# Attention and gated projection on one core: the second products of blocks 3 and 4 move to the end as seven block products for eight, with a new order

## The chip, the cores and the metric

The kernel runs on one core of one Trainium2 chip. The metric is the device time of one execution in microseconds (us), the median of several runs. The engines are named as in the profile: PE is TensorE, DVE is VectorE, ACT is ScalarE, POOL is GpSimd, SP is SyncE, which only issues transfers here.

## The reference

Two layers, all in fp32. The first is an attention whose weights are a sigmoid and not a softmax; the second multiplies a projection of its output with a gate, and projects again:

```
scores = q @ k.T / 8 - log(448)          # batch 8, 12 heads, 448 tokens, 64 per head
x      = sigmoid(scores) @ v             # then (8, 448, 768)
gate   = sigmoid(sum over k<5 of conv_w[k] * x shifted down by 4-k tokens)
out    = (gate * (x @ w_val)) @ w_out    # w_val, w_out: 768 x 768
```

## The kernel before, in words

**Attention.** The 96 heads are 48 *pairs*, and two pairs are one *two* (the index j, 24 of them; `TWOS`). Keys are cut in three chunks of 128 and a rest of 64. For a pair, `scores` (L592) gives three tiles of scores in PSUM, and `scores_rest` (L636) one tile with the rests of both pairs of a two. `attention` applies the sigmoid on ACT (L659); `attend` (L709 for the rests, L717 for the chunks) multiplies with the values. fp32 accuracy comes in one of two ways. A *whole* operand stays fp32, and each product is one fp32 matmul. A *split* operand is a high and a low part, and each product is three faster matmuls; the split of a tile of attention costs one more copy on ACT (L404 through `scaled`) and one subtraction on DVE (L670). `WHOLE` lists the twos whose attention is whole (0 to 8), `WHOLE_SCORES` the pairs whose scores are whole (0 to 14).

**Blocks.** Three twos make a *block*, one batch element: eight blocks, 0 to 7. Block 0 is cut in seven pieces of 64 tokens, one put behind each other block, so that the projections have seven blocks of 512 columns. `after` copies x out of PSUM on ACT, and makes the gate: five taps on ACT, DVE and POOL, the last two added by an accumulating transfer from POOL's queue (`gate<-tap`, L794). `x_split` makes a high and a low part of x (`xs`) with a scale for the block. In blocks none of whose twos is whole (`bounded`), the scale comes from exponents that are there early. In the others it comes from the largest x: `x_max` on DVE, a reduction, a small diagonal on ACT, and two matmuls by ones (`spread`, L813), which stand on PE ahead of the scores of a pair.

**The two projections.** `product("val", b, m)` (L864) is the first: for each of six m, 18 matmuls of 512 columns (six chunks, three terms), 108 in a block. DVE multiplies the result with the gate (`y`, L889 or L896). `product("out", b, m)` is the second, of the same size, with ACT's copy behind it (`y<-ps_m,o_scale`) and its stores; its operand `g` is a high part cast by a transfer from POOL's queue (`g<-y`, L898) and a low part by a subtraction (L409). This is how blocks 1 to 4 go. The blocks in `LATE` (5, 6, 7) are done in another way, at the end: y is written to HBM (`late_y`), loaded again in a tile of 2 x 2 quarters (`late_load`, ring `y4_ring` of one buffer; the trace names the load `y<-late_y`, L912), and `out_forms` makes seven combinations of the quarters, high and low (ring `f_ring` of one buffer; L923, L398, L409). `late_product` (L956) then does a 2 x 2 block product with seven products of half size in place of eight: four segments (`SEGMENTS`), 189 matmuls of 256 columns in a block, and puts the parts together (L404, L973, L968). Block 7 skips the way by HBM. The forms lie in rings of the attention that are free by then: `qk_src`, `qk_hi`, `qk_lo` for the first, third, ... block of `LATE`, the ring `a` for the second, fourth, ... So a block's forms can be made only when the products of the block two places ahead are done.

**The order.** Nothing is ordered by hand. `op(...)` records each operation with its engines, an estimated cost, a priority, what it reads and what it writes. `Plan.issue` then runs through a plan: on each engine the ready operation of the lowest priority goes first, and the instructions are emitted in that order, which on the chip is fixed for each engine. The priorities are made of the numbers of the table `AT`. An operation whose `port` is "VG" is planned so that DVE and POOL don't overlap in it; a POOL operation also waits on the chip for the last such DVE operation that was planned to take over 0.2 us.

Of the kernel before, what the change touches and what calls it, by code (L numbers as in the profile page):

```python
# [14 lines left out]
I32 = mybir.dt.int32  # L15
# [24 lines left out]
WHOLE = {*range(0, 9)}  # L40
WHOLE_SCORES = {*range(0, 15)}
# [40 lines left out]
LATE = (5, 6, 7)  # L82
AHEAD_OF_VAL = 3

FIRST_TOP = 6
SUMS = 12
OWN_BANKS = (6, 7)
# [5 lines left out]
BY_GPSIMD = ()  # L93
# [7 lines left out]
    first=-15.92, step=186.61, val=336.87, val_step=-29.39, out=-1237.15, out_step=257.57, w_max=1518.34,  # L101
    w_split=-860.95, load_qk_first=-201.47, load_qk=-1852.52, load_v=-662.01, split_hi=32.92, split_lo=-1097.78,
    rest_first=3174.29, rest=-1385.28, a_first=-2081.72, a=-74.73, attend=1686.54, v_max=-553.4, v_exp=-1453.48,
    v_split=144.91, x=-3266.86, x_max=-92.19, x_scale=515.03, x_hi=744.75, x_lo=177.24, x_step=2637.25,
    x_early=1120.5, first_max=-2492.59, tap=891.8, scores=8.56, a_rest=-659.37, a_rest_first=766.83,
    tap_first=-340.19, tap_pair=-743.04, tap_step=-330.6, gate=2823.26, product=-1112.74, y=2077.31, g_hi=-1119.86,
    g_lo=-3664.76, o=-3117.03, sums=-1119.35, f=-1154.59, late=-18.26, late_step=909.44, late_load=-912.54,
    pair0=2133.67, pair1=-1429.33, pair2=330.9, pair3=-1211.45, pair4=1377.13, pair5=-3156.16, pair6=297.98,
    pair7=-522.61, pair8=1609.62, pair9=-2397.11, pair10=-676.08, pair11=-98.56, pair12=-2966.57, pair13=-1287.04,
    pair14=1751.28, pair15=-717.37, pair16=545.19, pair17=-2818.83, pair18=-2085.26, pair19=495.26, pair20=75.11,  # L110
    pair21=-2539.24, pair22=-2144.55, pair23=158.2, val0=-2466.55, val1=1919.24, val2=208.28, val3=1536.8,
    val4=-2488.28, val5=-691.86, out0=173.81, out1=2060.89, out2=3408.9, out3=430.48, out4=2535.97, out5=-302.79,
    val_of1=-468.82, val_of2=-2362.91, val_of3=-1477.84, val_of4=1531.79, val_of5=1921.35, val_of6=-402.85,
    val_of7=1707.7, out_of1=-472.42, out_of2=247.7, out_of3=-1251.83, out_of4=-193.95, out_of5=1473.61,
    out_of6=-476.29, out_of7=-1672.61, share=2436.46, w_load=2736.66,
# [39 lines left out]
class Op:  # L155
    __slots__ = ("ways", "prio", "emit", "deps", "n", "start", "end", "eng", "after", "size", "port", "then")

    def __init__(self, n, ways, prio, emit, size, port):
        self.n, self.ways, self.prio, self.emit, self.size, self.port = n, ways, round(prio, 5), emit, size, port
        self.deps, self.after, self.then = set(), None, None  # L160
        self.start = self.end = self.eng = None


class Plan:
# [9 lines left out]
    YIELD = 0.3  # L174
    DMA_RATE = 310e3
# [5 lines left out]
    def op(self, ways, prio, emit, reads=(), writes=(), size=0, port="VG"):  # L181


        o = Op(len(self.ops), ways, prio, emit, size, port)
# [25 lines left out]
    def issue(self):  # L210
# [13 lines left out]
        events, order, bus, port = [], [], 0.0, 0.0  # L224
# [10 lines left out]
        while events:  # L235
# [6 lines left out]
            for e in engines:  # L242
# [19 lines left out]
                cost = o.ways[e]  # L262
                o.eng, o.start = e, t
# [24 lines left out]
def attention_then_gate(  # L288
# [59 lines left out]
    x_exp = ring(sb, 3, [P, 4], I32, "x_exp")  # L348
    o_scale = ring(sb, 3, [P, NC], F32, "o_scale")
# [9 lines left out]
    op = plan.op  # L359

# [70 lines left out]
    def exponent(e, read, cols, prio, po=None, top=V_TOP):  # L431
# [4 lines left out]
        op({"V": 0.06}, prio + 0.2, lambda _: nc.vector.tensor_scalar(  # L436
            cols[0](), cols[0](), float(31 << 23), float(254 << 23), op0=ALU.max, op1=ALU.min), [], e)
        op({"V": 0.06}, prio + 0.4, lambda _: nc.vector.tensor_scalar(
# [27 lines left out]
    def weight_split(n, m, po=None, to=None):  # L466
# [3 lines left out]
        if po is None:  # L470
            po = ps_m.new()
            to = lambda: po()
            reads, emit = weight_sum(n, m)
            op({"P": 0.05}, prio - 1, lambda e: emit(to()), reads, [po])
# [3 lines left out]
        op({"V": 0.06}, prio, lambda _: nc.vector.tensor_scalar(  # L478
# [102 lines left out]
    def scores(i, c, sums=()):  # L581
# [13 lines left out]
        cost = (0.755 if i in WHOLE_SCORES else 0.607) + (0.1 if c != 1 else 0) + (0.09 if c == 0 and i % 2 else 0) + 0.06 * len(sums)  # L595
        return op({"P": cost}, tau(i) + AT["scores"], emit,
                  (sources(i)[:1] if i == c == 0 else sources(i)) + [x for reads, _ in sums for x in reads], [b])
# [4 lines left out]
    def x_bound(b, t):  # L602
# [6 lines left out]
        op({"V": 0.08}, t + 0.1, lambda _: nc.vector.tensor_scalar(  # L609
            col(0), bits(x), bits(y), bits(z), op0=ALU.max, op1=ALU.max), [x, y, z], [e])  # L610
        op({"V": 0.08}, t + 0.2, lambda _: nc.vector.tensor_scalar(
            col(0), col(0), bits(first_top), float(254 << 23), op0=ALU.max, op1=ALU.min), [first_top], [e])
        op({"V": 0.06}, t + 0.3, lambda _: nc.vector.tensor_scalar(
            col(1), col(0), -1.0, float((254 + X_TOP) << 23), op0=ALU.mult, op1=ALU.add), [], [e])

    def scores_rest(j):
# [12 lines left out]
        def emit(e):  # L629
# [4 lines left out]
            for n, to in enumerate(halves):  # L634
# [3 lines left out]
        o = op({"P": (0.99 if m else 0.89) + (0.1 if firsts else 0)}, t + AT["rest_first" if 2 * j < AHEAD else "rest"], emit,  # L638
               [q for n in range(2) for q in st[2 * j + n]["qk_all"]] + ([ones, m] if m else []) + firsts, [b])
        if firsts:  # L640
            op({"V": 0.08}, t + AT["v_exp"], lambda _: nc.vector.tensor_scalar(
                first_top()[:, 1:4], b()[:, 0, S + 1 : S + 4].bitcast(I32), 0x7F800000, None, op0=ALU.bitwise_and), [], [b, first_top], port="")
            op({"V": 0.08}, t + AT["v_exp"] + 0.1, lambda _: nc.vector.tensor_scalar(
# [552 lines left out]
```

## Time and profile before

| | |
|---|---|
| time, median of 3 runs (lowest, highest) | 575.81 us (575.28, 576.5) |
| the profiled execution's own time | 575.5 us |
| span of that execution, first to last instruction | 573.6 us |
| PE busy | 563.7 us, 98% of the span |
| DVE, ACT, POOL busy | 74%, 70%, 42% |
| granted TensorE clock, mean | 0.998 |
| moved by DMA | 107.25 MB, mean 187 GB/s |

How to read it: the span is 1.9 us shorter than the time of the same execution, and the rest lies around the span. All sums in the prediction are made against 575.5 us. A PE matmul shows a duration longer than its step, since matmuls are pipelined; the step is read from the start of one to the start of the next, or from a piece of the chain divided by its count. The same holds for ACT and DVE: the duration of an instruction holds some 0.1 us in which the next one runs already. A row of the chain "7.77 PE ps_m L864 x36" is 36 matmuls that took 7.77 us on the path that ended last. Whole (fp32) matmuls are recorded twice each, so a pair of whole scores (6 matmuls) is a row with x12.

### The profile page before, as it was taken

To read this page: it belongs to the slowest core of one execution; us is meant where nothing else is said; L and a number is where in the kernel's file an instruction comes from. 1 tells how busy PE (TensorE), PEld (TensorE's weight loads), DVE (VectorE), ACT (ScalarE), POOL (GpSimd) and SP (SyncE) were. 2 spreads that over 40 slices of the span, in tenths; PEclk is the share of its full clock that TensorE was granted. 3 is DMA by queue.
4 is the path that set the end of the run, shared out by engine and by line. 5 is a ranking of instruction groups with operands and counts; after the bars stand their busy time and mean duration, and the time that the engine had idled before them with its cause. 6 is when DMAs were issued, how large, how long until landed. Compare 5 with 4: busy or idle time off the path is not lost.

```text
span 573.6 us, 9982 instructions
## 1 busy us (share of the span) xinstructions
PE 563.7 (98%) x3793; PEld 300.6 (52%) x3793; DVE 423.6 (74%) x653; ACT 401.6 (70%) x488; POOL 242.6 (42%) x301
## 2 busy tenths in 40 slices
PE   9999989999999999999999999999999999999996
PEld 4343334454554545545455445455555446865785
DVE  0867998896789775486766778866878999847544
ACT  5788986556987859677686878997889994332221
POOL 0001346866656285365734455545665421400100
PEclk9999999999999999999999999999999999999999
DMA  8987789968586979686495775976787565730122
GB/s 312 360 272 247 223 216 229 218 159 230 186 207 201 300 162 246 161 198 155 109 231 146 205 172 152 219 191 184 204 237 197 137 166 143 188 94 14 61 75 74
DMA packets 48400, 107.25 MB, mean 187 GB/s; under 512 B 15712, under 2 KB 24544, under 8 KB 48352
## 3 DMA queue, kind: packets, MB, share of 16 engines
q1 hardware_dynamic: 33808, 67.19, 34.3%
q0 software_dynamic: 14256, 39.23, 33.6%
q8 instruction: 30, 0.49, 0.3%
q10 hardware_dynamic: 288, 0.20, 0.1%
q14 instruction: 18, 0.15, 0.1%
HBM read 63.52 MB, written 17.90 MB: 142 GB/s over the span
## 4 chain that ended last, share of the span: by engine, by line
PE 89%; ACT 4%; DVE 3%; issue 2%; DMA 1%; POOL 1%; DVEq 0%; ACTq 0%
PE ps_m L864 42%; PE ps_a L592 15%; PE ps_a L717 15%; PE late L956 7%; PE ps_m L956 4%; PE ps_a L636 4%; PE ps_a L709 3%; ACT a_single L659 1%; DMA g<-y 1%; DVE a L670 1%; ACT gate L404 1%; PE ps_m L1023 1%; DVE gate L790 0%; POOL w_form L409 0%; DVE y L896 0%
## 5 line engine op out<-in xcount | busy, mean ns | idle before, releaser
L864 PE MATMUL ps_m<-xs,w_val_hi 128*128 128x512 f16 x504 | 150.1, 379 | 0.6 <-DVE y L896 0.6
L670 DVE SCALAR_TENSOR_TENSOR a<-ps_a,a 128x896 f16<-128x896 f32 x90 | 95.1, 1090 | 29.2 <-ACT a L404 29.0
L659 ACT ACTIVATE ps_a<-ps_a 128x896 f32<-128x896 f32 x105 | 93.2, 911 | 26.6 <-DVE v_exp L649 16.1
L864 PE MATMUL ps_m<-xs,w_val_lo 128*128 128x512 f16 x252 | 95.5, 379 | 0.0
L787 POOL TENSOR_SCALAR tap<-x,cw 128x512 f32<-128x512 f32 x84 | 69.2, 845 | 56.6 <-DVE gate L790 14.1
L409 POOL TENSOR_TENSOR qk_lo<-qk_src,qk_hi 128x448 fp32r<-128x448 f32 x66 | 74.9, 1156 | 29.9 <-DVE gate L790 11.1
L864 PE MATMUL ps_m<-g,w_out_hi 128*128 128x512 f16 x288 | 86.0, 380 | 0.5 <-POOL g L409 0.5
L404 ACT ACTIVATE a<-ps_a 128x896 f16<-128x896 f32 x90 | 80.1, 928 | 0.2
L864 PEld LDWEIGHTS <-w_val_hi 128*128 128x128 f16 x504 | 47.6, 98 | 60.0 <-issue 7.8
L790 DVE SCALAR_TENSOR_TENSOR gate<-x,cw,gate 128x512 f32<-128x512 f32 x84 | 65.3, 798 | 0.5 <-ACT gate L404 0.3
L659 ACT ACTIVATE a_single<-ps_a 128x896 f32<-128x896 f32 x63 | 53.6, 928 | 17.0 <-DVE out_inverse L434 8.5
L794 POOL DMA_DIRECT2D gate<-tap x42 | 38.8, 925 | 50.3 <-DMA gate<-tap 25.4
L864 PE MATMUL ps_m<-g,w_out_lo 128*128 128x512 f16 x144 | 54.6, 379 | 0.0
L717 PE MATMUL ps_a<-a,v_hi 128*64 128x448 f16 x360 | 49.4, 355 | 0.0
L864 PEld LDWEIGHTS <-w_out_hi 128*128 128x128 f16 x288 | 27.0, 98 | 35.0 <-issue 4.3
L717 PE MATMUL ps_a<-a_single,v_src 128*64 128x448 f32 x216 | 42.6, 543 | 0.0
L567 POOL DMA_DIRECT2D qk_hi<-qk x33 | 20.8, 630 | 48.4 <-PE ps_a L592 35.8
L592 PE MATMUL ps_a<-qk_hi 64*128 64x448 f32 x198 | 40.1, 401 | 0.8 <-DVE a_rest L670 0.8
L864 PEld LDWEIGHTS <-w_val_lo 128*128 128x128 f16 x252 | 24.7, 98 | 29.7
L592 PE MATMUL ps_a<-qk_single 64*128 64x448 f32 x180 | 37.2, 553 | 0.2 <-ACT a_single L659 0.2
L592 PE MATMUL ps_a<-qk_lo,qk_hi 64*128 64x448 f32 x198 | 36.3, 362 | 0.0
L592 PE MATMUL ps_a<-qk_hi,qk_lo 64*128 64x448 f32 x198 | 36.3, 362 | 0.0
(144 smaller groups left out, 936.4 us busy)
## 6 DMA issues: line engine op xcount, KB each, us to landing
gate<-tap POOLq DMA_DIRECT2D x42, 512.0 KB, 5.8
qk_src<-qk SPq DMA_DIRECT2D x33, 448.0 KB, 5.0
qk_hi<-qk POOLq DMA_DIRECT2D x33, 416.0 KB, 4.3
v_src<-vs SPq DMA_DIRECT2D x24, 448.0 KB, 4.1
qk_single<-qk SPq DMA_DIRECT2D x14, 448.0 KB, 6.2
out_t<-y SPq DMA_DIRECT2D x24, 224.0 KB, 2.1
w_words<-w_val SPq DMA_DIRECT2D x6, 768.0 KB, 7.9
w_words<-w_out SPq DMA_DIRECT2D x6, 768.0 KB, 4.8
```

Of the source, the lines that this page charges most:

```text
L404: nc.scalar.activation(to, x, AF.Copy, scale=by)
L409: engines[eng].tensor_tensor(to, x, y, op=ALU.subtract)
L592: mm(b()[:, h, :S], k()[rows, at : at + P], q()[rows, :S], start=(n == 0), stop=(n == len(terms(i)) - 1))
L636: mm(b()[to, h, :S], x[n]()[rows, CW:], x[n]()[rows, :S], start=True, stop=True)
L659: nc.scalar.activation(to, b()[:, :, :S], AF.Sigmoid, bias=-math.log(S), scale=1.0 / math.sqrt(D))
L670: op({"V": 1.0}, t + 0.5, lambda e: nc.vector.scalar_tensor_tensor(part(1), p(), A_SCALE, part(0), op0=ALU.mult, op1=ALU.subtract), [b], [ ...
L717: mm(px()[to, p, :S], v()[:, o : o + D], x(st[2 * j + p]["a", c])[:, h, at : at + S], start=(j == 0 and c == 0 and n == 0), stop=(j > 0 an ...
L787: op({"G": TAP_G}, at + AT["tap_step"] * k - AT["tap_first"] + AT["tap_pair"] * p, lambda e, p=p, k=k, tap=tap: nc.gpsimd.tensor_scalar(by ...
L790: op({"V": 0.67}, at + AT["tap_step"] * k + AT["tap_pair"] * p, lambda e, p=p, part=part, k=k: nc.vector.scalar_tensor_tensor(part(), x()[ ...
L794: op({"G": 1.1}, at + AT["tap_step"] * k, lambda e, tap=tap: nc.gpsimd.dma_start(g(), tap(), accum_op=ALU.add), [tap], [g], 4 * P * T * 4, "")
L864: mm(po()[:, cs], w()[:, c, :], x(k)[:, cs], start=(c == 0 and j == 0), stop=(c == NC - 1 and j == 2))
L956: mm(po()[:, i * HT : (i + 1) * HT], weights(w, k, c), gv[b, c][g]()[:, x, :], start=(c == 0 and i == 0 and j == 0), stop=(c == UNITS - 1 ...
```

## The change

- `LATE` grows from blocks 5 to 7 to blocks 3 to 7. `product("out")` is left for blocks 1 and 2. Segments of the first late block use ring `ps_m`, all others `ps_a`; before, that was block 5, now block 3.
- Two 13 (in block 4) becomes whole, and so do the scores of pair 16 (in two 8). Block 4 is thereby no longer `bounded`: its scale comes from the largest x.
- One-column DVE operations get `port=""` (`narrow`): the plan no longer keeps them apart from POOL. POOL operations now wait for the last DVE operation with `port="VG"` of any planned length.
- The plan's costs on PE change by some hundredths of a us, and changing from one shape of matmul to another gets a cost of its own (`form`, `LEAVE`, `ENTER`).
- Three weights listed in `BY_GPSIMD` get their low half in another way: ACT scales in place and copies, and DVE or POOL subtracts.
- The rings `x_exp` and `o_scale` have 8 buffers, not 3. All numbers of `AT` are new.

```diff
-WHOLE = {*range(0, 9)}
-WHOLE_SCORES = {*range(0, 15)}
+WHOLE = {*range(0, 9), 13}
+WHOLE_SCORES = {*range(0, 15), 16}
...
-LATE = (5, 6, 7)
+LATE = (3, 4, 5, 6, 7)
 AHEAD_OF_VAL = 3
+FIRST_OUT = min({*range(1, B)} - {*LATE}, default=B - 2)
-OWN_BANKS = (6, 7)
...
-BY_GPSIMD = ()
+BY_GPSIMD = (("out", 3), ("out", 5), ("val", 3),)
...
-    first=-15.92, step=186.61, val=336.87, val_step=-29.39, out=-1237.15, out_step=257.57, w_max=1518.34,
+    first=1564.19, step=536.35, val=1468.75, val_step=6875.3, out=4116.12, out_step=3023.8, w_max=-13597.73,
...
+    LEAVE = {"full": 0.0, "wide": 0.095, "tall": 0.098, "small": 0.0}
+    ENTER = {"full": 0.008, "wide": 0.1, "tall": 0.03, "small": 0.0}
...
+                if e == "P":
+                    if o.form != form:
+                        cost += self.LEAVE[form] + self.ENTER[o.form]
+                    form = o.form
...
-    x_exp = ring(sb, 3, [P, 4], I32, "x_exp")
-    o_scale = ring(sb, 3, [P, NC], F32, "o_scale")
+    x_exp = ring(sb, 8, [P, 4], I32, "x_exp")
+    o_scale = ring(sb, 8, [P, NC], F32, "o_scale")
...
+    def narrow(*of):
+        return op(*of, port="")
...
-        op({"V": 0.06}, prio + 0.2, lambda _: nc.vector.tensor_scalar(
+        narrow({"V": 0.06}, prio + 0.2, lambda _: nc.vector.tensor_scalar(
...
-            po = ps_a.new(lambda: ps.tile([P, 512], F32, name="late", tag="ps_a", bufs=ps_a.n)) if b in OWN_BANKS else ps_m.new()
+            po = ps_a.new(lambda: ps.tile([P, 512], F32, name="late", tag="ps_a", bufs=ps_a.n)) if b != LATE[0] else ps_m.new()
...
-        if b == 2:
+        if b == FIRST_OUT + 1:
             weight_scales("out")
-            x_unscale(1)
-        if b > 1:
+            for n in range(1, b):
+                x_unscale(n)
+        if b > FIRST_OUT:
...
-            elif o.eng == "V" and o.ways["V"] > 0.2:
+            elif o.eng == "V":
                 last = traced
```

Counted in the order of the two kernels, on PE: matmuls of 512 columns by `w_out` go from 432 to 216, matmuls of 256 columns of the late products from 567 to 945. On ACT the copies `y<-ps_m,o_scale` go from 24 to 12, the copies of late parts from 18 to 30, the casts of forms from 18 to 30. On POOL's queue the casts `g<-y` go from 24 to 12. On SP's queue the writes of `late_y` go from 12 to 24, the loads of them from 6 to 12.

What moves is seen at three places. **ACT in the second half of the attention**, behind the copy of two 18's x; before (`a` is a split tile of attention, `ps_a` the sigmoid in place, `y` the copy behind a second product):

```order
L404 ACTIVATE v_hi<-v_src,v_exp 128x896
L404 ACTIVATE a<-ps_a 128x2x448
L404 ACTIVATE y<-ps_m,o_scale 128x512
L404 ACTIVATE gate<-x,cw 128x512
L659 ACTIVATE ps_a<-ps_a 128x2x448 x2
L404 ACTIVATE a<-ps_a 128x2x448 x2
L404 ACTIVATE y<-ps_m,o_scale 128x512
L659 ACTIVATE ps_a<-ps_a 128x2x448
L404 ACTIVATE gate<-x,cw 128x512
L404 ACTIVATE a<-ps_a 128x2x448
L796 ACTIVATE gate<-gate 128x1024
L404 ACTIVATE y<-ps_m,o_scale 128x512
```

and in the change, at the same place:

```order
L415 ACTIVATE v_hi<-v_src,v_exp 128x896
L415 ACTIVATE a<-ps_a 128x2x448
L807 ACTIVATE gate<-gate 128x1024
L670 ACTIVATE ps_a<-ps_a 128x2x448 x2
L415 ACTIVATE a<-ps_a 128x2x448 x2
L670 ACTIVATE ps_a<-ps_a 128x2x448
L415 ACTIVATE gate<-x,cw 128x512
L415 ACTIVATE a<-ps_a 128x2x448
L415 ACTIVATE gate<-x,cw 128x512
L670 ACTIVATE ps_a<-ps_a 128x2x448
L415 ACTIVATE xs<-x,x_exp 128x1024
L415 ACTIVATE a_rest<-ps_a 128x2x448
```

The copies of second products are gone from here, and the same work of the attention stands closer together.

**PE ahead of the scores of pair 31** (in two 15), where block 4 ends; before, a second product stands there:

```order
L864 MATMUL ps_m<-g_2885,w_out_hi_96 128x512
L864 LDWEIGHTS w_out_lo_108
L864 MATMUL ps_m<-g_2885,w_out_lo_108 128x512
L592 MATMUL ps_a<-qk_hi 128x448 x2
L592 MATMUL ps_a<-qk_hi,qk_lo 128x448 x2
```

and in the change a first product, and then the two matmuls by ones of block 4's scale:

```order
L875 LDWEIGHTS w_val_lo_107
L875 MATMUL ps_m<-xs,w_val_lo_107 128x512
L824 LDWEIGHTS ones
L824 MATMUL ps_a<-diagonal,ones 128x64
L824 LDWEIGHTS ones
L824 MATMUL ps_a<-diagonal,ones 128x64
L603 MATMUL ps_a<-qk_hi 128x448 x2
L603 MATMUL ps_a<-qk_hi,qk_lo 128x448 x2
```

The scores of pair 31, and all that follows on PE, now stand behind `diagonal`, which ACT makes.

**SP's queue at the end**; before (the second number of `late_y` is the third of the projection, the last one the tensor: 72 to 74 are block 5, 75 to 77 block 6):

```order
L912 DMA y_4950<-late_y_1_73 128x1024
L891 DMA late_y_0_75<-y 128x512 x2
L912 DMA y_5112<-late_y_2_74 128x1024
L891 DMA late_y_1_76<-y 128x512 x2
L912 DMA y_5219<-late_y_0_75 128x1024
L891 DMA late_y_2_77<-y 128x512
L912 DMA y_5287<-late_y_1_76 128x1024
L891 DMA late_y_2_77<-y 128x512
L1001 DMA out_t<-parts 128x2x448
L1001 DMA out_t<-parts 128x2x64
L912 DMA y_5434<-late_y_2_77 128x1024
```

and in the change (72 to 74 are block 3, 75 to 77 block 4, 78 to 80 block 5, 81 to 83 block 6):

```order
L923 DMA y_4966<-late_y_1_76 128x1024
L1012 DMA out_t<-parts 128x2x448
L1012 DMA out_t<-parts 128x2x64
L923 DMA y_5115<-late_y_2_77 128x1024
L1012 DMA out_t<-parts 128x2x448
L1012 DMA out_t<-parts 128x2x64
L923 DMA y_5207<-late_y_0_78 128x1024
L1012 DMA out_t<-parts 128x2x448
L1012 DMA out_t<-parts 128x2x64
L1012 DMA out_t<-parts 128x2x448
L1012 DMA out_t<-parts 128x2x64
L923 DMA y_5329<-late_y_1_79 128x1024
```

The loads now alternate with the stores of finished products: a block's y is loaded while the block before it is being multiplied.

## Rows read from the trace of the kernel before

**Rows 1.** The page: busy time, share of the span and instructions of each engine, and the granted TensorE clock in 40 slices (9 is 90% or more).

```profile
PE 563.7 (98%) x3793; PEld 300.6 (52%) x3793; DVE 423.6 (74%) x653; ACT 401.6 (70%) x488; POOL 242.6 (42%) x301
...
PEclk9999999999999999999999999999999999999999
```

**Rows 2.** All waits of PE: what waited, for whom, us in total, times, the longest.

```profile
PE ps_a L813 <- ACT diagonal L404: 1.3, 1, 1.3
PE ps_m L1023 <- DVE ones L1016: 1.1, 1, 1.1
PE ps_a L592 <- DVE a_rest L670: 0.8, 1, 0.8
PE ps_m L864 <- DVE y L896: 0.6, 1, 0.6
PE ps_m L864 <- POOL g L409: 0.5, 1, 0.5
PE ps_a L633 <- ACT a_single L659: 0.3, 1, 0.3
PE ps_a L636 <- ACT a_single L659: 0.3, 1, 0.3
PE ps_a L592 <- ACT a_single L659: 0.2, 1, 0.2
```

**Rows 3.** The chain that ended last, from 60 to 92 us, in order of time: start, us, what. L709 and L717 are the whole attend of a two, L592 x12 the whole scores of a pair.

```profile
68.04 0.75 PE ps_a L709 x8
68.79 4.68 PE ps_a L717 x24
...
86.75 2.46 PE ps_a L592 x12
```

**Rows 4.** The same chain from 400 to 455 us: one two of the split attention, from its rest scores (L636) to the next.

```profile
412.43 0.91 PE ps_a L636 x8
413.34 0.57 PE ps_a L709 x12
413.91 3.53 PE ps_a L717 x36
417.44 2.03 PE ps_a L592 x18
419.46 5.29 PE ps_m L864 x24
424.75 2.03 PE ps_a L592 x18
426.78 2.70 PE ps_m L864 x12
...
429.48 0.91 PE ps_a L636 x8
```

**Rows 5.** The same chain from 505 to 574 us: 36 matmuls of 512 columns, 276 late matmuls of 256 columns, and what follows PE's last.

```profile
509.37 7.77 PE ps_m L864 x36
...
538.25 30.27 PE late L956 x276
...
568.54 0.75 DVE parts L968
```

**Rows 6.** PE in order of time, about 77 and 309 us: start, us, engine, line, operation, [idle before, and what ended it].

```profile
77.38 0.22 PE L813 MATMUL ps_a<-diagonal,ones 128*128 128x64 bf16 x2 [1.29 <-ACT diagonal L404]
77.53 0.65 PE L592 MATMUL ps_a<-qk_single 64*128 64x448 f32 x2
...
309.12 0.17 PE L631 MATMUL ps_a<-vm,ones 128*128 128x1 bf16 x1
309.21 0.98 PE L636 MATMUL ps_a<-qk_src 64*64 64x448 f32 x8
```

**Rows 7.** Three stretches: length, busy time and instructions of PE, PEld, DVE, ACT and POOL, granted clock, DMA's share, GB/s. The first is six twos of the split attention, from rest scores to rest scores; the second the densest stretch of ACT; the third the late products beside the rest of the first products.

```profile
331.67:447.95 116.28, 116.28 (x841) 61.22 (x844) 90.32 (x132) 101.57 (x123) 66.01 (x82) 1.00 0.76 196
439.67:472.82 33.15, 32.33 (x214) 16.46 (x216) 31.27 (x44) 32.80 (x40) 13.27 (x17) 1.00 0.61 158
472.82:538.25 65.43, 65.43 (x476) 43.79 (x465) 44.88 (x72) 21.68 (x27) 10.01 (x11) 1.00 0.39 101
```

**Rows 8.** ACT's groups in the first of these stretches (331.67 to 447.95 us): busy us, mean ns, idle before them and what ended it.

```profile
L659 ACT ACTIVATE ps_a<-ps_a 128x896 f32<-128x896 f32 x42 | 37.3, 913 | 9.4 <-DVE v_exp L649 6.4 <-PE ps_a L592 2.9
...
L404 ACT ACTIVATE x<-ps_a,v_exp 128x896 f32<-128x896 f32 x6 | 6.0, 1006 | 5.3 <-PE ps_a L717 5.3
...
L404 ACT ACTIVATE y<-ps_m,o_scale 128x512 f32<-128x512 f32 x6 | 4.2, 695 | 0.1
```

**Rows 9.** The loads of late y on SP's queue in order of time, 460 to 500 us.

```profile
467.96 0.32 SPq L912 DMA_DIRECT2D y<-late_y  x1
...
476.88 0.32 SPq L912 DMA_DIRECT2D y<-late_y  x1
...
484.65 0.32 SPq L912 DMA_DIRECT2D y<-late_y  x1
...
494.99 0.34 SPq L912 DMA_DIRECT2D y<-late_y  x1
```

**Rows 10.** Two groups of DVE over the whole span: a six-column operation with `port="VG"`, and a one-column one.

```profile
L831 DVE TENSOR_SCALAR o_scale<-o_base,x_exp 128x6 f32<-128x6 f32 x7 | 6.0, 857 | 0.1
...
L829 DVE TENSOR_SCALAR x_exp<-x_exp 128x1 f32<-128x1 f32 x7 | 1.0, 145 | 0.0
```

More of the change, by code (lines that the diff above doesn't have):

```diff
@@ new lines @@
+    w_split=4887.09, load_qk_first=19087.91, load_qk=22652.0, load_v=-10027.13, split_hi=1393.39, split_lo=-2273.26,
+    rest_first=28009.33, rest=-1368.78, a_first=-13044.74, a=-15086.09, attend=-22955.31, v_max=-10769.23,
+    v_exp=-31213.73, v_split=-3170.55, x=-22099.28, x_max=18978.65, x_scale=1030.85, x_hi=6026.59, x_lo=8531.41,
+    x_step=5071.56, x_early=6465.83, first_max=11567.01, tap=1132.59, scores=13759.23, a_rest=-17835.52,
+    a_rest_first=10628.9, tap_first=10241.68, tap_pair=742.46, tap_step=-1737.78, gate=7569.71, product=3755.81,
@@ L155, with __init__ @@
 class Op:
-    __slots__ = ("ways", "prio", "emit", "deps", "n", "start", "end", "eng", "after", "size", "port", "then")
-    def __init__(self, n, ways, prio, emit, size, port):
+    __slots__ = ("ways", "prio", "emit", "deps", "n", "start", "end", "eng", "after", "size", "port", "then", "form")
+    def __init__(self, n, ways, prio, emit, size, port, form):
         self.n, self.ways, self.prio, self.emit, self.size, self.port = n, ways, round(prio, 5), emit, size, port
+        self.form = form
         self.deps, self.after, self.then = set(), None, None
@@ L179, in __init__, with op @@
         self.ops = []
-    def op(self, ways, prio, emit, reads=(), writes=(), size=0, port="VG"):
-        o = Op(len(self.ops), ways, prio, emit, size, port)
+    def op(self, ways, prio, emit, reads=(), writes=(), size=0, port="VG", form="full"):
+        o = Op(len(self.ops), ways, prio, emit, size, port, form)
         self.ops.append(o)
@@ L223, in issue @@
         held = dict.fromkeys(engines)
-        events, order, bus, port = [], [], 0.0, 0.0
+        events, order, bus, port, form = [], [], 0.0, 0.0, "full"
         def release(o, t):
@@ L636, in emit @@
                     mm(b()[to, h, :S], x[n]()[rows, CW:], x[n]()[rows, :S], start=True, stop=True)
-        o = op({"P": (0.99 if m else 0.89) + (0.1 if firsts else 0)}, t + AT["rest_first" if 2 * j < AHEAD else "rest"], emit,
-               [q for n in range(2) for q in st[2 * j + n]["qk_all"]] + ([ones, m] if m else []) + firsts, [b])
+        o = op({"P": (0.9 if m else 0.805) + (0.09 if firsts else 0)}, t + AT["rest_first" if 2 * j < AHEAD else "rest"], emit,
+               [q for n in range(2) for q in st[2 * j + n]["qk_all"]] + ([ones, m] if m else []) + firsts, [b], form="small")
         if firsts:
@@ L719, in chunks @@
                            skip_group_check=True)
[L721 removed]
+        steps = [op({"P": 0.861 if single else 0.677}, t, rest, [s["a"], *values], [px], form="small")] if j else []
         for p in range(2):
             for cs in ((0, 1), (2,)):
[L724 removed]
+                cost = (0.752 if single else 0.567) * len(cs)
                 steps.append(op({"P": cost}, t, lambda e, p=p, cs=cs: chunks(p, cs),
[L726 removed]
+                                [*(st[2 * j + p]["a", c] for c in cs), *values], [px], form="tall"))
         if not j:
[L728 removed]
+            steps.append(op({"P": 0.861}, t, rest, [s["a"], *values], [px], form="small"))
         for a, b in zip(steps, steps[1:]):
```

62 lines of the change are left out of this document (27 added, 35 removed).

## The prediction

> **What bounds the kernel now.** I read the page first: PE is busy 98% of the span at full clock, every other engine at most 74% [rows 1]. A busy PE alone proves nothing, since matmuls overlap in it, so the second view is the list of PE's waits. All eight together are 5.1 us [rows 2], of which 1.1 is the start. PE thus stands still for 4.0 us of 573.6 once it runs. The third view is the chain in order of time, which gives the price of PE's work in steps, free of the overlap [rows 3 to 5]. The reader is to see that time here is PE's work plus a few waits: what PE no longer has to do is gained, unless new waits take it back. So the sum has two halves: what the change does to PE's work, and who could be late where PE's work gets less.
>
> **The sum**, against the profiled execution's 575.5 us (0.3 under the median of the three, 575.81).
>
> *Second products of blocks 3 and 4.* 432 less 216 is 216 matmuls of 512 columns gone. 36 of them take 7.77 us [rows 5], 0.2158 each, so 46.6 us go. 945 less 567 is 378 late matmuls of 256 columns added. 276 take 30.27 us [rows 5], 0.1097 each, so 41.5 us come. Net **-5.1**. Eight products of the old size would have been 432 in place of 378: the 54 that are missing are the gain, less a little because two matmuls of 256 columns cost 0.219 and one of 512 costs 0.216.
>
> A rule speaks against this. The Trainium skill ("TensorE: Matmul & The Clock Gate", section "Back-to-back issue gap") gives for a sustained stream some 81 ns a matmul of 128 columns and 131 ns of 512. Between them an estimate from that page is some 98 ns for 256 columns, three quarters of the long one and not half, by which the two blocks would lose 8.8 us and not gain 5. The rows above decide against it here: the ratio is 0.1097 to 0.2158.
>
> *Pair 16 with whole scores.* 2.46 us [rows 3] for 2.03 [rows 4]: **+0.4**. It saves POOL a split and a transfer; POOL is not on the path there.
>
> *Two 13 whole.* Its attend takes 0.75 + 4.68 [rows 3] for 0.57 + 3.53 [rows 4]: +1.3. The small matmul for the largest v goes, 0.09 by the starts 309.12 and 309.21 [rows 6]: **+1.2** together. ACT and DVE lose some seven copies and seven subtractions there; it is one two, and cover, not path.
>
> *Block 4's scale.* Two matmuls by ones, 0.15 by the starts 77.38 and 77.53, **+0.15**. They also stand ahead of pair 31's scores, behind a chain from the last x of the block over DVE and ACT. Of the two such places now one waits 1.29 us [rows 6] and the other not at all [rows 2]; those are the bounds, and I take the mean, **+0.65**. Queued behind them is all of PE.
>
> *Edits that I price at nothing.* The order on PE changes its shape of matmul about as often as before, so no switching time is added or saved. One-column DVE operations took 145 ns already, against 857 for the six-column one that keeps `port="VG"` [rows 10]: the chip did not hold them back, so freeing them in the plan moves places in the order, no duration. POOL's added waits on short DVE operations stand on an engine that is busy 42% [rows 1]. The three weights of `BY_GPSIMD` add a copy of under 1 us each on ACT, early, beside PE; if that cover were gone, up to 1 us each. More scale buffers only remove waits. On POOL's queue twelve casts `g<-y` go. On SP's, twelve writes and six loads come and 24 stores of y go against twelve of parts; all are covered by PE's work, the loads with the exception below.
>
> Without new waits: 575.5 - 5.1 + 0.4 + 1.2 + 0.15 + 0.65 = 572.8.
>
> **The attention gets denser: the disputed term.** While the attention lasts, second products were filler for PE in which ACT and DVE could catch up. With blocks 3 and 4 gone, the order has 288 first-product matmuls in the eight twos from the attend of two 15 to that of two 23, 36 each. The last full two of [rows 4] has just that, 24 and 12, and takes 17.05 us (412.43 to 429.48). The six twos of the first stretch take 19.4 us each now [rows 7]. ACT's work in them is 101.57 / 6 = 16.9 us a two, of which 4.2 / 6 = 0.7 are second products' copies that go [rows 8]: 16.2 us of 17.05, **95%**. DVE has 90.32 / 6 = 15.1 (88%), POOL 11.0 (65%), DMA 76% of a longer time [rows 7]. Nothing exceeds PE, but ACT has only 0.85 us a two to wait in.
>
> What that costs is bounded thus. From below: nothing, for PE was busy in all of 116.28 us with ACT at 87%, and one two at the new density is among them. From above: the densest stretch, ACT 32.80 of 33.15 us, where PE lost 0.82 [rows 7]; over 8 x 17.05 = 136.4 us that is 3.4 us, of which 0.8 is in the time already, so +2.6. ACT's 95% lies nearer to the dense stretch. But casts of forms stood in the queue there, and most of these come later in the new order, so I take **+0.5**.
>
> **The end.** The late products need their forms. A block's three sets are made one after the other, through one buffer for y and one for f. The loads of y were issued at 467.96, 476.88, 484.65 and 494.99 [rows 9], 7.8 to 10.3 us apart, 9.0 in the mean. Block 5's sets can start when block 3's products are done, and have as cover block 4's 189 late matmuls (20.7 us) and, by the order, 39 of the first products (8.4 us), 29.1 together. Three sets take 23 to 31 us, 27 in the mean: covered, with up to 1.8 us open. Block 6's have block 5's products and 72 first-product matmuls, 36 us. ACT and DVE are no limit there, at 33% and 69% in the third stretch [rows 7]. I take nothing. After PE's last matmul the same work follows as now [rows 5].
>
> Forecast: 572.8 + 0.5 = **573.3 us**, 2.5 under the median.
>
> **The rivals.**
> - *ACT becomes the bound in the eight twos* (slower). For it: ACT idled 14.7 / 6 = 2.45 us a two in the first stretch, 1.07 of that waiting for DVE's exponent of v, 1.4 for PE [rows 8]. If ACT must wait over 0.85 us a two, it sets the pace. With only the 1.07 a two takes 17.3. With all 2.45 it takes 18.65, 1.6 more eight times, 12.8 us in all. With half of that, 0.8 a two, the time is 572.8 + 6.4 = 579.2. Against it: waits for PE shrink when PE is no longer ahead, and ACT ran 33 us with hardly a gap [rows 7]. Slower than before from 0.5 us a two on. Chance 0.15.
> - *The forms come late* (about no change). Each set costs 10.3 us, as the slowest did, and block 5's products wait 1.8 us; with the upper bounds of the dense stretch half taken, 572.8 + 1.8 + 1.3 = 575.9. Single y loads were never this often on the path, and the loads now stand behind stores in SP's queue, each waiting for a product. Chance 0.16.
> - *Long matmuls are cheaper by the column than the short ones* (the page's rule). At three quarters of 0.2158, 0.162, 378 cost 61.2 us and the net is +14.6 and not -5.1: 593. The late stretch at 0.1097 rules it out. Chance 0.01.
> - *The new order also removes waits.* The waits of [rows 2] stand at seven places whose neighbours all move. If half of the 4.0 us and block 4's wait go, 572.8 - 2.0 - 0.65 - 0.15 = 570.0. It is on the forecast's side; chance 0.15.
> - That the change doesn't do what it says is excluded by the counts in the order (945 and 216).
>
> **How the numbers follow.** Forecast within its bounds 0.53, fewer waits 0.15: faster **0.68**, where faster means over 0.2%, 1.15 us, about what a measurement can tell here. Late forms 0.16: **same**. ACT 0.15 and the page's rule 0.01: slower **0.16**. The range goes down to 570.3, near the case with fewer waits, and up to 577.3, past the late forms (575.9) and both upper bounds of the sum (572.8 + 0.65 + 2.6 = 576.1), short of most of ACT's case.
>
> **What the next profile would show.** Right: the L875 group of `w_out` falls to 216 matmuls and the late ones rise to 945 at the same steps (0.216 and 0.11). The late stretch, from the last attend on, lasts some 150 us and has no PE wait over 1 us. PE's waits total 4 to 6.5 us, and ACT is over 93% busy from about 285 to 420 us. Wrong: PE's waits over 9 us. If they are on ACT or on `a`'s subtraction between 285 and 420 us, the first rival is right, if on the forms after that, the second. If PE's work itself, without waits, doesn't fall by about 3.3 us, the prices are wrong.

## The result: 1% slower, and the profile after

The changed kernel takes 581.82 us, the kernel before 575.75 on the same chip: ratio 1.0103, interval 1.008 to 1.0126. The forecast was 573.3, with a range up to 577.3. The profiled execution took 582.57 us, 7.1 more than that of before.

First the page after: busy time by engine, and the granted clock in 40 slices. It answers to [rows 1].

```profile
PE 565.1 (97%) x3934; PEld 315.3 (54%) x3934; DVE 442.0 (76%) x691; ACT 407.6 (70%) x496; POOL 243.0 (42%) x294
...
PEclk9999999999999999999989999999999999999999
```

PE's busy time didn't fall, although work was taken from it. But busy PE hides steps that are longer than usual, so the steps come next. The chain after, from 504 to 560 us (start, us, what), answers to [rows 5]:

```profile
503.95 15.28 PE late L967 x140
519.23 7.77 PE ps_m L875 x36
...
536.41 23.69 PE late L967 x217
```

0.1091 and 0.1092 us a late matmul of 256 columns, 0.2158 one of 512: the prices of the forecast, and the counts are as forecast. Then all waits of PE, which answer to [rows 2]:

```profile
PE ps_a L603 <- DVE a L681: 2.8, 2, 1.7
PE ps_a L824 <- ACT diagonal L415: 2.1, 1, 2.1
PE ps_a L647 <- ACT a_single L670: 1.5, 1, 1.5
PE ps_m L875 <- DVE y L900: 1.1, 3, 0.4
PE ps_m L1034 <- DVE ones L1027: 1.1, 1, 1.1
PE ps_m L967 <- DVE parts L979: 0.6, 1, 0.6
PE ps_m L967 <- ACT parts L415: 0.5, 1, 0.5
PE ps_a L603 <- ACT a_single L670: 0.4, 1, 0.4
PE ps_a L603 <- DVE a_rest L681: 0.2, 1, 0.2
PE ps_m L967 <- DVE y L900: 0.2, 1, 0.2
```

10.5 us in all, where [rows 2] has 5.1. To split the time fully I add up, from the starts in the trace, what each of PE's steps takes beyond the usual step of its kind, where that is 0.07 us or more. These are the *stalls*; the rest of the time from PE's first matmul to its last is its *work*:

| us | first to last | work | stalls | to 100 us | 100 to 270 | rest of the attention | behind it |
|---|---|---|---|---|---|---|---|
| before | 567.5 | 561.8 | 5.6 | 3.0 | 0.7 | 1.9 | 0.1 |
| after | 574.3 | 559.2 | 15.2 | 5.6 | 0.2 | 6.5 | 2.8 |

The attention ends at 476 us before and 429 after; the border between the last two columns is put at 475 and 432 us. **The work fell by 2.6 us, where 3.35 was forecast (-5.1 + 0.4 + 1.2 + 0.15); the stalls rose by 9.5, where 1.15 was.**

The longest stall of the attention, in PE's order of time (start, us, operation, [idle before, and what ended it]):

```profile
292.95 0.37 PE L603 MATMUL ps_a<-qk_lo,qk_hi 64*128 64x448 f32 x2
295.06 0.47 PE L603 MATMUL ps_a<-qk_hi 64*128 64x448 f32 x2 [1.74 <-DVE a L681]
...
295.86 1.03 PE L875 MATMUL ps_m<-xs,w_val_hi 128*128 128x512 f16 x2
296.69 0.63 PE L875 MATMUL ps_m<-xs,w_val_lo 128*128 128x512 f16 x1
297.12 1.06 PE L875 MATMUL ps_m<-xs,w_val_hi 128*128 128x512 f16 x2
```

The third tile of a pair's scores waits for a place in PSUM, which is free when DVE has subtracted the split of an older tile. Behind the wait the first products go at 0.43 us a matmul, twice the usual step: the clock stands at its lower level, 1.2 GHz, for some 3 us. The row of that stretch (PE, PEld, DVE, ACT, POOL, granted clock, DMA, GB/s) and that of PE's first wait for y:

```profile
296.00:297.00 1.00, 1.00 (x3) 0.30 (x2) 1.00 (x2) 1.00 (x2) 0.61 (x2) 0.50 0.71 274
435.60:450.12 14.52, 13.59 (x74) 6.97 (x72) 14.33 (x18) 5.59 (x7) 6.73 (x9) 1.00 0.78 188
```

The low clock adds 1.6 us to the wait. In the other row DVE is busy 99%, half of it with the gate's taps:

```profile
L801 DVE SCALAR_TENSOR_TENSOR gate<-x,cw,gate 128x512 f32<-128x512 f32 x8 | 7.1, 904 | 0.0
```

Beside these 7.1 us it has 4.0 of splits of x, 3.0 of y and 1.1 of combinations for the first late block, and y, for which PE waits, stands in this queue.

What led to the wait at 293 us is seen in the chain before it:

```profile
289.00 0.90 DVE xs L854
...
290.12 0.59 DVE a L681
...
291.12 1.08 DVE a L681
292.19 0.66 DVE y L900
292.85 0.42 DVE v_lo L701
293.27 0.56 issue
293.83 1.09 DVE a L681
294.93 0.14 issue
295.06 0.87 PE ps_a L603 x6
```

DVE goes from splits of x to subtractions, y and the low part of v. The "issue" at 293.27 isn't idle time of DVE: by the timeline it works on the low part of v until the last subtraction starts. ACT's copy for that subtraction came first (start, us):

```profile
292.27 0.93 ACT L415 ACTIVATE a<-ps_a 128x896 f16<-128x896 f32 x1
292.77 1.14 DVE L701 SCALAR_TENSOR_TENSOR v_lo<-v_src,v_exp,v_hi 128x896 f16<-128x896 f32 x1
```

The copy was done at 293.20 and the subtraction began at 293.83. So some 0.6 us of the wait is DVE's queue; how much of the rest is ACT's isn't seen here.

### The profile page after: what moved, and what is told of

The parts are those of the page before. It is cut to its first block, busy times and chain, and to the rows that moved or that the text cites. A ratio compares the mean times of both kernels' runs of the same rounds, so it can differ in the third digit from the quotient of the medians.

```text
span 580.8 us, 10312 instructions
## 1 busy us (share of the span) xinstructions
PE 565.1 (97%) x3934; PEld 315.3 (54%) x3934; DVE 442.0 (76%) x691; ACT 407.6 (70%) x496; POOL 243.0 (42%) x294
## 4 chain that ended last, share of the span: by engine, by line
PE 73%; DVE 10%; ACT 10%; issue 4%; DMA 1%; POOL 0%; DVEq 0%; ACTq 0%; SPq 0%
PE ps_m L875 26%; PE late L967 14%; PE ps_a L603 12%; PE ps_a L728 12%; ACT ps_a L670 4%; PE ps_a L647 3%; ACT a L415 3%; PE ps_m L967 2%; DVE a L681 2%; PE ps_a L720 2%; DVE gate L801 2%; DVE y L900 1%; DMA y<-late_y 1%; ACT gate L415 1%; DVE forms L420 1%
## 5 line engine op out<-in xcount | busy, mean ns | idle before, releaser
L681 DVE SCALAR_TENSOR_TENSOR a<-ps_a,a 128x896 f16<-128x896 f32 x84 | 88.8, 1085 | 27.5 <-ACT a L415 27.4
L670 ACT ACTIVATE ps_a<-ps_a 128x896 f32<-128x896 f32 x98 | 87.7, 920 | 14.4 <-DVE v_exp L660 11.3
L415 ACT ACTIVATE a<-ps_a 128x896 f16<-128x896 f32 x84 | 74.9, 936 | 0.0
L670 ACT ACTIVATE a_single<-ps_a 128x896 f32<-128x896 f32 x70 | 59.2, 927 | 11.1 <-PE ps_a L720 4.4
L967 PE MATMUL late<-forms,w_form 128*128 128x256 f16 x432 | 58.0, 273 | 0.0
L967 PEld LDWEIGHTS <-w_form 128*128 128x128 f16 x540 | 52.8, 98 | 8.1 <-issue 0.7
L415 ACT ACTIVATE parts<-late,o_scale 128x512 f32<-128x512 f32 x24 | 16.4, 687 | 47.9 <-PE late L967 47.9
L984 DVE TENSOR_TENSOR parts<-parts 128x256 f32<-128x256 f32 (+1 forms) x58 | 27.2, 491 | 27.4 <-ACT parts L415 26.9
L875 PE MATMUL ps_m<-g,w_out_hi 128*128 128x512 f16 x144 | 42.9, 379 | 0.0
L967 PE MATMUL late<-forms,w_out_hi 128*128 128x256 f16 x216 | 38.8, 273 | 0.0
```

The lines of the kernel that those rows point to most:

```text
L415: nc.scalar.activation(to, x, AF.Copy, scale=by)
L670: nc.scalar.activation(to, b()[:, :, :S], AF.Sigmoid, bias=-math.log(S), scale=1.0 / math.sqrt(D))
L681: op({"V": 1.0}, t + 0.5, lambda e: nc.vector.scalar_tensor_tensor(part(1), p(), A_SCALE, part(0), op0=ALU.mult, op1=ALU.subtract), [b], [ ...
L875: mm(po()[:, cs], w()[:, c, :], x(k)[:, cs], start=(c == 0 and j == 0), stop=(c == NC - 1 and j == 2))
L967: mm(po()[:, i * HT : (i + 1) * HT], weights(w, k, c), gv[b, c][g]()[:, x, :], start=(c == 0 and i == 0 and j == 0), stop=(c == UNITS - 1 ...
L984: op({"V": 0.07 + 0.00104 * k, "G": 0.1 + 0.0021 * k}, t, lambda e: engines[e].tensor_tensor(to(), x(), z(), op=ALU.add), reads, [buf])
```

## The experiments

Three theories: **O**, the new order makes the waits, and another order is free of them; **D**, the attention has become too dense for ACT and DVE; **P**, short DVE operations now hold POOL back. The kernel before, measured beside each run, took 575.2 to 575.8 us.

### POOL's waits

e4 undoes the last edit of the diff alone; the order stays.

```diff
-            elif o.eng == "V":
+            elif o.eng == "V" and o.ways["V"] > 0.2:
                 last = traced
```

> The changed kernel in its own order, where POOL operations wait for the last DVE operation that was planned over 0.2 us, as before the change, and no longer for short ones. Theory P: the waits of POOL delay taps and low parts, and the time falls by 2 to 6 us. Theories O and D: POOL is busy 42% and not in front of PE; the time stays within 0.7 us.

582.4 us (1.0119, interval 1.0101 to 1.0138), the waits as in the changed kernel. P falls.

### Operations moved at single places

e1, e2, e3 and e7 emit the planned list with a few operations at other places:

```diff
-    for o in plan.issue():
+    for o in moved(plan.issue()):
```

e1 moves ten (two first taps behind sigmoids, `diagonal` ahead of a sigmoid, the exponents ahead of taps, x's copy earlier), e2 20, e3 19, e7 two (`v_hi` and `v_lo` at 291 to 294 us), e11 those of e1, e2 and e3 together, but for two (47).

> The changed kernel, with ten operations of ACT, DVE and POOL in the first 100 us issued at other places (casts of weights and taps behind the sigmoids and behind the scale of block 1); PE's order and all work stay. Theory O (the lost time is waits that the new order makes, each at its place): the waits on the diagonal (2.1 us) and on the rest scores (1.5 us) fall below 1 us together, and the time falls by 2.0 to 3.5 us against the changed kernel. Theory D (only the thinner cover of the attention behind 285 us costs time): it falls by under 1 us, since a gain so early is waited away later. Theory P (short DVE operations that now hold POOL cost the time): no change, within 0.7 us.

> The changed kernel, with 20 operations of ACT, DVE and POOL between 255 and 432 us at other places (splits of x, taps and low parts of v behind the attention's own subtractions); PE's order and all work stay. Theory O: the waits of scores on a's subtraction (1.7 and 1.1 us) go, the clock holds at 1.00 behind 295 us, and the time falls by 3.5 to 6 us: 3 to 4 of waits and 1.7 of the low clock. Theory D: ACT and DVE are short of time in this stretch whatever their order, the waits turn up at other pairs, and the time falls by 0 to 1.5 us. Theory P: no change, within 0.7 us.

> The changed kernel, with 19 operations of ACT, DVE and POOL between 425 and 480 us at other places (y's product ahead of the splits of x and the taps, the parts' copy ahead of the forms); PE's order and all work stay. Theory O: the waits on y (1.1 us), on the first forms and on the parts (1.6 us) shrink to about 1 us, and the time falls by 1.5 to 3 us. Theory D: it falls by under 1 us, since the places lie behind the dense stretch and its delay remains. Theory P: no change, within 0.7 us.

> The changed kernel with two operations moved, both at its longest wait after 100 us, that of scores on a's subtraction at 293 to 295 us: on ACT the high part of v (v_hi) and on DVE its low part (v_lo) are issued behind the third split of a and no longer ahead of it. Theory O: the wait of 1.7 us falls below 0.5 us, the low clock behind it goes, and the time falls by 1.5 to 3.3 us. Theory D: this wait shrinks, but what was passed over is late at the next products with v or the next scores; the time falls by under 0.7 us.

> The changed kernel with the moves of the early, the middle and the late place together (47 operations of ACT, DVE and POOL; PE and SP keep their order). Theory O: the three gains add up: 1.9 + 1.8 + 0.4 us gives 577.7 us, and up to 2 us more where a wait that one of them pushed on is taken away by the next; 575.5 to 578. Theory D: the middle keeps its wait of about 1.7 us and its low clock, and the time stays at 578 us or above.

| | us | ratio, interval | stalls: to 100 us | 270 to 432 | behind |
|---|---|---|---|---|---|
| changed | 581.82 | 1.0103, 1.008 to 1.0126 | 5.6 | 6.5 | 2.8 |
| e1 | 579.88 | 1.0082, 1.0068 to 1.0095 | 4.7 | 4.9 | 2.8 |
| e2 | 580.04 | 1.0086, 1.0069 to 1.0103 | 6.6 | 5.3 | 2.6 |
| e3 | 581.43 | 1.0101, 1.0085 to 1.0116 | 5.7 | 5.1 | 3.2 |
| e7 | 580.97 | 1.0093, 1.008 to 1.0106 | 5.8 | 5.0 | 2.9 |
| e11 | 581.22 | 1.0117, 1.0095 to 1.0139 | 7.6 | 5.3 | 3.2 |

No interval lies clear of the changed kernel's. Against its median e1 gains 1.9 us, just short of theory O's range, e2 1.8, between the two theories, and e3 0.4, as D expected. The named waits of e1 did shrink where they were aimed at; PE's waits in e1:

```profile
PE ps_a L628 <- DVE a L706: 2.8, 2, 1.8
PE ps_a L628 <- ACT x L434: 1.9, 1, 1.9
...
PE ps_a L672 <- ACT a_single L695: 0.6, 1, 0.6
PE ps_a L849 <- ACT diagonal L440: 0.5, 1, 0.5
```

3.6 us on the diagonal and the rest scores became 1.1, but a new wait of 1.9 on a copy of x stands some 10 us later. By the chain, that copy needs a place in x's ring, which DVE frees with the split of an older x, and this stands behind its taps and the casts of weights. e2 missed the wait at 293 us (1.7 again) and cut that at 385 to 0.2. e7 cut the one at 293 to 0.7, and 0.6 turned up three us later, on PE's small matmul for the largest v (the 1.1 in the first row is the wait at 384 us, which e7 left alone):

```profile
PE ps_a L627 <- DVE a L705: 1.8, 2, 1.1
294.11 0.47 PE L627 MATMUL ps_a<-qk_hi 64*128 64x448 f32 x2 [0.69 <-DVE a L705]
...
PE ps_a L666 <- DVE a L705: 0.6, 1, 0.6
```

The stall of 1.91 us became 0.85 + 0.79. The stretch gained more (1.5 us), since the low clock followed the wait on the diagonal here and is in the first column. That most of the delay only moved is D's expectation; the time fell by 0.85 us, between D's 0.7 and O's 1.5, and not clear of the noise. In e3 the waits on y went (1.1 to 0.4), and the one on the parts' copy grew from 0.5 to 1.6. e11 shows that the gains don't add: its profiled execution has two stretches of low clock.

### Whole orders made anew

e5 and e6 replace the order of both kernels by one in which, by the durations of their traces, fewer operations wait; in e9 and e10 only ACT and DVE change, by five places at most.

> The changed kernel with all its operations, issued in another order on PE, ACT, DVE and POOL over the whole span (found by moving operations a few places so that, with the durations of the trace, fewer wait). SP's queue keeps its order. Theory O (the lost time is the order's, and the smaller work of PE is there to be had): PE's waits fall from 10.3 to under 4 us, the low clock at 295 us goes, and the time is 568 to 573 us, under the kernel before. Theory D (with the second products of blocks 3 and 4 gone, ACT and DVE can't keep up from 285 to 430 us in any order): waits of 3 to 5 us and the low clock stay there, and the time is 575 to 579 us.

> The kernel before, its order treated in the same way with the durations of its own trace. Both theories: its waits of 5.1 us fall to under 3 us and its time by 2 to 5 us, to 571 to 573.5 us. Theory O: the changed kernel treated so lies 1 to 3.5 us below this one, by the work that PE no longer has. Theory D: it lies above this one by 3 us or more.

> The changed kernel with all its operations; PE, POOL and SP keep their order, so that no transfer from POOL's or SP's queue changes places, and ACT and DVE issue theirs at most five places earlier or later (127 of 496 and 253 of 689 moved, so that by the trace's durations fewer wait). Theory O: the waits at 76 to 84 us, at 293 and 385 us and at 438 to 470 us shrink from 10 us together to 4 us or less, and the time is 569 to 574 us, below the kernel before. Theory D: about 3 us of waits stay between 285 and 430 us, those outside go, and the time is 575 to 578 us. If the moves only push the waits on, as in the reordering that also moved POOL and PE, the time is above 580 us.

> The kernel before, treated in the same way: PE, POOL and SP keep their order, ACT and DVE issue theirs at most five places earlier or later by its own trace's durations. Both theories: its 4 us of waits inside the run shrink to 1 to 2 us, and the time is 571 to 574 us. Theory O: the changed kernel treated so lies within 2 us of this one or below it. Theory D: it lies 3 us or more above it.

621.9, 606.0, 591.5 and 590.4 us (ratios 1.082, 1.054, 1.0285 and 1.0247): all far slower, and they decide nothing between O and D. Moving POOL's operations moved its transfers. In e5 the low parts of q and k wait for their high parts' transfer, 19 times:

```profile
POOL qk_lo L550 <- DMA qk_hi<-qk: 62.9, 19, 7.0
```

In e9 and e10 no transfer changes its place in its queue; why they lose as much isn't shown.

### Less work for DVE

e8 skips, in the same order, the 41 taps that DVE adds between 262 and 445 us:

```diff
     for o in plan.issue():
+        if o.n in SKIP:
+            continue
         o.emit(o.eng)
```

> The changed kernel in its own order without the 41 taps that DVE adds to the gate between 262 and 445 us (33 us of DVE; the gate lacks them). PE, ACT and POOL keep their work. Theory D, with DVE as the short engine: the waits on a's subtraction (2.8 us) and on y (1.1 us) and the low clock go, and the time falls by 4 to 6 us. With ACT as the short engine: only the waits that DVE's queue made by itself go, and the time falls by 0.5 to 2.5 us. Theory O says the same as the second: what is left waits for ACT in its order.

579.74 us (1.0071, interval 1.0058 to 1.0084). Its row of 285 to 425 us has DVE at 73% and ACT at 94%, and the waits on `a` are still there:

```profile
285.00:425.00 140.00, 136.72 (x1017) 71.97 (x1015) 102.60 (x150) 131.50 (x160) 80.75 (x101) 1.00 0.78 205
```

```profile
PE ps_a L608 <- DVE a L686: 3.0, 3, 1.6
...
PE ps_m L880 <- DVE y L905: 0.4, 1, 0.4
```

So DVE's taps don't make these waits. What stands ahead of the subtraction that ends the longest of them:

```profile
292.23 0.93 ACT L420 ACTIVATE a<-ps_a 128x896 f16<-128x896 f32 x1
292.50 1.14 DVE L706 SCALAR_TENSOR_TENSOR v_lo<-v_src,v_exp,v_hi 128x896 f16<-128x896 f32 x1
293.56 1.08 DVE L686 SCALAR_TENSOR_TENSOR a<-ps_a,a 128x896 f16<-128x896 f32 x1
```

ACT's copy was done at 293.16, so 0.4 of the 1.6 us is the low part of v on DVE, and the rest points to ACT, which worked without a gap from 287.24 us on. The stalls behind the attention fell from 2.8 to 1.2 us, and those were DVE's queue.

### Parts of the change alone, and other densities

Here the order is planned anew from the table's numbers. e12 is the kernel before with `LATE = (3, 4, 5, 6, 7)` and what this needs; e13 and e17 are the changed kernel with three and four late blocks, e14 without two 13 and pair 16 whole, e15 and e16 with one two more whole (e15 to e17 in two executions each). The edit of e13:

```diff
-LATE = (3, 4, 5, 6, 7)
+LATE = (5, 6, 7)
```

> The kernel before with one part of the change alone: the second products of blocks 3 and 4 go to the end as well (LATE of five blocks, the rings and scales that this needs); numbers, costs and the whole twos stay as they were, and the order follows from the old numbers. PE's work falls by 5.1 us. Theory D: without that filler ACT and DVE are late all over the second half of the attention, and the time is 578 to 590 us. Theory O: the new numbers made the loss; with the old ones waits rise by less than 5 us and the time is 570 to 576 us.

> The changed kernel with three late blocks (5 to 7), as before the change, and all its other edits and numbers. PE has 5.1 us of work more, and the second products of blocks 3 and 4 are back as filler. Theory D: the waits between 285 and 430 us go, and the time is 576 to 581 us, below the changed kernel in spite of the longer work. Theory O: the new numbers make waits here too, and the time is 583 to 592 us.

> The changed kernel without two 13 and pair 16 among the whole ones: PE's work is 1.7 us shorter by the rows of before (0.4 + 1.2 + 0.15), ACT and DVE have seven more copies and subtractions about 340 us, and the order follows from the same numbers. Theory D: ACT has even less time there, waits rise by more than PE saves, and the time is 581 to 586 us. Theory O: the time is 577 to 581 us, or anything if the order falls out otherwise.

> The changed kernel with two 14 whole as well (in block 4, whose scale comes from the largest x already). PE +1.2 us, ACT and DVE seven copies and seven subtractions less just ahead of the dense stretch. If relief of ACT there is what counts (theory D), the waits on a's subtraction fall below the 2.8 us of the changed kernel and the time is 578 to 582 us. If what counts is that the numbers were made for one set of operations (theory O), they rise to over 8 us and the time is 588 to 598 us, as for the other kernels whose order followed anew from the numbers.

> The same with two 17 in place of two 14 (in block 5, which thereby takes its scale from the largest x: two matmuls by ones more). PE +1.4 us, ACT's relief lies inside the dense stretch. Theory D: 577 to 582 us. Theory O: 588 to 600 us.

> The changed kernel with four late blocks (4 to 7): the second product of block 3 is back as filler, PE has 2.55 us of work more. By theory D ACT's share in 285 to 425 us falls from 93% to about 88% and the waits on a's subtraction to about what the kernel with three late blocks had (3.5 us) or less. By theory O the time is 585 to 600 us all the same, with waits elsewhere; by theory D alone it is 576 to 583 us.

The stretch from 285 to 425 us, in the kernels before, after and e12 (columns as above):

```profile
285.00:425.00 140.00, 139.36 (x987) 72.57 (x980) 101.65 (x147) 115.69 (x141) 70.02 (x91) 1.00 0.75 192
```

```profile
285.00:425.00 140.00, 136.90 (x1001) 71.42 (x997) 122.61 (x176) 129.88 (x157) 82.76 (x100) 0.99 0.78 201
```

```profile
285.00:425.00 140.00, 127.86 (x959) 66.22 (x953) 118.27 (x176) 132.57 (x160) 79.96 (x101) 0.95 0.79 207
```

ACT goes from 83% to 93% and 95%. All of them side by side, by late blocks:

| | late | us | work | ACT, 285 to 425 | waits on `a` | stalls 270 to 432 | behind 432 |
|---|---|---|---|---|---|---|---|
| before | 3 | 575.75 | 561.8 | 83% | none | 1.9 to 475 us | 0.1 |
| e13 | 3 | 600.52 | 564.0 | 83% | 3.5 | 3.9 | 17.6 |
| e17 | 4 | 584.89 | 561.1 | 87% | 3.4 | 7.0 | 1.8 |
| after | 5 | 581.82 | 559.2 | 93% | 2.8 | 6.5 | 2.8 |
| e16, two 17 whole | 5 | 586.56 | 560.2 | 84% | 2.9 | 7.8 | 3.6 |
| e15, two 14 whole | 5 | 591.54 | 560.7 | 91% | 6.4 | 14.0 | 2.4 |
| e14, two 13 split | 5 | 594.47 | 558.2 | 90% | 10.3 | 14.4 | 3.6 |
| e12, old numbers | 5 | 595.62 | 556.9 | 95% | 12.6 | 20.4 | 3.7 |

All six lie above the range that theory D gave them. Four things follow. *The work is as forecast*: two blocks more at the end take 4.9 us off PE (561.8 to 556.9) and 4.8 with the new numbers (564.0 to 559.2). *Five late blocks bring waits on `a` with the old numbers too.* In e12, PE waits for it eleven times:

```profile
PE ps_a L592 <- DVE a L670: 12.6, 11, 1.9
```

and this kernel, which differs from the one before in the number of late blocks and the order that follows, loses 20.4 us of stalls in that stretch for 1.9. *The new numbers aren't better by themselves*: with three late blocks, and ACT at 83%, they stall for 17.6 us at the end, the longest behind forms:

```profile
PE ps_m L967 <- DVE forms L420: 2.9, 2, 2.0
PE late L967 <- ACT forms L409: 2.7, 2, 1.7
```

*ACT's share of the whole stretch doesn't tell where PE waits.* e13, e16 and e17 have ACT at 83 to 87% and as much waiting for `a` as the changed kernel at 93%. What goes with the waits is how many products of 512 columns PE has in one two, counted from rest scores to rest scores, from 255 us on, in the eight kernels of the table. Each of the 21 twos with 33 or fewer has over 1 us of waits; of the eight with 36, five have none; of the 32 with 42 or more, 30 have under 0.4 us. The kernel before has no two under 36. Three twos of the changed kernel, its products alone (length, PE and PEld with counts, granted clock, DMA, GB/s):

```profile
281.70:298.50 16.80, 6.05 (x21) 2.12 (x21) 0.92 0.69 187
336.30:353.05 16.75, 8.03 (x36) 3.34 (x36) 1.00 0.90 229
372.00:389.20 17.20, 7.31 (x33) 3.06 (x33) 1.00 0.82 210
```

The first and the third hold its two waits on `a` (1.74 and 1.09 us); the second, like the other with 36 (from 389 us), has none. No run changed this number alone, and e2, with 33 in the third, has 0.2 us there, so the order on ACT and DVE counts too.

O is right in that every order of e12 to e17 loses 15 to 28 us of stalls: the numbers fit the very operations for which they were made. How much of the changed kernel's own 6.5 us another order could save stays open, since none that was tried came under the kernel before.

## Why the prediction was wrong, point by point

- **Second products of blocks 3 and 4, -5.1**: right, -4.9 and -4.8 in the two pairs of kernels, at 0.109 and 0.216 us a matmul. The rule of the Trainium skill ("TensorE: Matmul & The Clock Gate", section "Back-to-back issue gap") that the forecast weighed doesn't agree with these steps.
- **Two 13 and pair 16 whole, +1.75 with the scale's matmuls**: too large, the work of after less that of e14 is +1.0. Whether ACT's and DVE's copies of this two were "cover, not path" isn't shown: e14, without the whole two, takes 594.47 us, but its order was planned anew, and e15, with one whole two more, loses nearly as much.
- **Block 4's scale, the mean of 0 and 1.29**: neither matmul waits in the new order. But the like place of block 1, at 77 us before and 79 now, waits 2.05 for 1.29 us and the rest scores behind it 1.52 for 0.25. On ACT a tap of 0.7 us now stands ahead of the sigmoids in front of `diagonal`, and on DVE 3.1 us of taps stand ahead of the reduction behind it. The forecast had no term for the first 100 us, where the order also changed, and weighed of the new order only that it removes waits; 2.7 us.
- **The denser attention, +0.5 with +2.6 as upper bound**: this is the step that failed. The share was right (95% forecast, 93% found, 95% in e12), the price was not: 4.6 us. The forecast spread the 288 products evenly, "36 each". The mean is right, and twos with 36 take 17.05 to 17.15 us without a wait, as in [rows 4]. But the order gives one two 21 and another 33, and their waits (1.74 and 1.09) and the low clock behind the first (1.6) are 4.4 of the 6.5 us of stalls. The upper bound came from 33 us in which ACT was as busy, but with casts of forms for which no wait of [rows 2] stands. Whether another spread of the same products would be free of waits stays open.
- **The end, nothing**: 2.8 us. The forms through the single buffers were in time, as forecast. What was late is y, the parts' copy and their subtraction while block 3's segments share the two buffers of `ps_m` with the first products; DVE, 69% busy in the like stretch of before [rows 7], is at 99% there. No single wait of this stretch is over 0.6 us, which the forecast's sign (none over 1 us) let pass.
- **The rivals**: "ACT becomes the bound in the eight twos", at 579.2 with a chance of 0.15, names the largest loss, and e8 points to ACT and not to DVE's taps. It came at 4.6 us for 6.4, and two smaller losses came on top. The signs given for it also came: 10.5 us of waits, over 9, and 2.8 of them on `a` between 285 and 420 us.

Together: -2.6 of work, and +2.7, -0.5, +4.6 and +2.7 of stalls, make +6.9 from PE's first matmul to its last. Of the work, -4.9 and +1.0 leave 1.3 us that only kernels with the new numbers and the small edits have (558.2 in e14, 556.9 in e12); which steps they are wasn't traced.

## What to carry to other kernels

Work that is taken from a bound engine in the middle of a program is also cover for those that feed it: count in the new order, stretch by stretch and not in the mean, how much of it is left. Here a two with 36 products in the changed kernel cost nothing, and in all eight kernels each with 33 or fewer waited over 1 us, while ACT's share of the whole stretch didn't tell them apart. An order that a planner made fits one set of operations; each edit here that was planned with numbers made for another cost 3 to 20 us against the kernel they were made for, so parts of such a change can't be priced alone by their time, only by the work and the waits in their traces.

## What the runs showed of the hardware

A wait of about 2 us was often, but not always, followed by some 3 us at the lower clock (0.50). Of the changed kernel and its close relatives, the changed one, e2 and e4 have it behind the wait at 293 us, e3 and e7 behind that at 77 to 82 us, e11 behind two waits, and e1 and e8, with waits as long at 293 us (1.8 and 1.6), nowhere. Summed over the longer steps it costs 1.5 to 1.6 us in the first three. The Trainium skill ("TensorE: Matmul & The Clock Gate", section "A second HAM failure mode: psum-queue depth-cycling") tells of a kernel whose clock went down again and again by short idle times of PE between groups of matmuls. These rows agree only in part: a single wait comes before each low clock here, and there are at most two in one of these executions.
